# Taking half of the query-major exponentials from DMA transposes in an attention gradient kernel

## The chip, the cores and the metric

The kernel runs on one core of one Trainium2 chip. The metric is device microseconds of one execution. The kernel before takes 2852.1 us (median of 2 runs, 2850.25 to 2853.94). "PE" is the matmul engine, "DVE" the vector engine, "ACT" the activation engine, "POOL" the general one, and "SP" the engine whose queue issues the transposes. A busy DMA share can exceed 1, because it adds up the times of overlapping packets.

## The reference

The program is a forward pass and its gradients: `out = x + attention(LN(x)) * silu(mlp(LN(x)))`, with 2048 tokens, width 512, 32 heads of 16. The part that matters is the attention and its backward pass:

```
p  = softmax(q k^T / 4)          # 2048 x 2048, for each of 32 heads
o  = p v
dV = p^T do
dS = p * (do v^T - rowsum(do*o)) # the backward pass of the softmax
dQ = dS k ,  dK = dS^T q
```

The exponentials are wanted in two layouts. Sums over keys (o, dQ) need key-major tiles, with keys on the partitions. Sums over queries (dK, dV) need query-major ones. The same number is therefore wanted twice, transposed.

## The kernel before

The attention part works through 16 pairs of heads times 4 chunks of 512 queries, which makes 64 blocks of 16 steps. In a step `g`:

- PE computes key-major scores `s` (128 keys x 512 queries, two heads), and ACT computes `et = exp(s)`.
- PE computes `d`, and DVE multiplies it with `et` into `gts`. Every two steps a 512 KB DMA transpose turns `gts` into the query-major `gk`.
- For a *unit* of the block before (128 queries x 512 keys, two heads; `kc` is the group of 512 keys, `qb` the group of 128 queries), the query-major exponentials come by one of two ways. Either PE computes the transposed scores `t` and ACT a second exp, `e = exp(t)`; or a 256 KB DMA transpose of a part of `et` delivers `ek`. The list `dma_units` says which. PE then multiplies them, and `gk`, into `Z`.

```python
    dma_units = ((1, 3), (3, 3))          # (kc, qb): 2 of a block's 16 units
    lagb = 3
    ...
    ps_st = ...tc.tile_pool(name="ps_st", bufs=2, space=PSUM)   # s and t share two buffers
    etp = sb("etp", 3)
    gtp = sb("gtp", 4)
    gbp = sb("gbp", 6)                    # gk tiles, 8 KB a partition each
    ekp = sb("ekp", 4)                    # ek tiles, 2 KB a partition each
    ...
    def emit_t(g):
        b = b_unit(g)
        if b is None or b[1:] in dma_units:
            return                        # no scores and no second exp for these
        ...
    def emit_dmat(g):
        ...
        if kb % 2 == 1:
            h = (kb // 2) % 2
            if h == 0:
                blk[j]["Gk"][kc] = gbp.tile([128, 2, 16, 128], bf16, name="gk")
            nc.sync.dma_start_transpose(out=blk[j]["Gk"][kc][:, h], in_=st_gt[g][:].rearrange("k a h q -> k (a h q)"))
        if kb % 4 == 3:
            for qb in range(4):
                if (kc, qb) in dma_units:
                    ek = ekp.tile([128, 8, 128], bf16, name="ek")
                    blk[j]["Ek"][(kc, qb)] = ek
                    nc.sync.dma_start_transpose(out=ek[:], in_=st_et[g][:, qb].rearrange("k a h q -> k (a h q)"))
    ...
    def emit_z(g, part):                  # the unit of block j, one block and lagb steps later
        ...
            if (kc, qb) in dma_units:
                ev = blk[j]["Ek"].pop((kc, qb))[:].rearrange("q (a h) k -> q h a k", h=2)
            else:
                ev = st_e.pop(g)[:].rearrange("q h (a k) -> q h a k", a=4)
            for hj in range(2):
                nc.tensor.matmul(Z[...], lhsT=blk[j]["W1"][:, qb, hj, :], rhs=ev[:, hj], ...)
    ...
    for g in range(NSTEP + 16 + lagb):    # the whole loop is unrolled
        ...
        emit_t(g); emit_le(g - 1); emit_exp_b(g); emit_s(g + 1); emit_d(g)
        emit_mult(g); emit_exp_a(g + 1); emit_dmat(g); emit_g(g - 1)
        emit_z(g - lagb, 0); emit_z(g - lagb, 1)
```

## Time and profile before

| | |
|---|---|
| span of the profiled run | 2849 us |
| attention loop | 287 to about 2240 us |
| a step, a block | 1.90 us, 30.4 us |
| exps per block | 16 key-major, 14 query-major |
| DMA transposes per block | 8 gk (512 KB), 2 ek (256 KB) |
| moved by DMA in the loop | 171 GB/s, 5.2 MB a block |

The page of the kernel before gives the span in 40 slices: busy tenths of ACT and DMA, the clock granted to PE, and the GB/s moved.

```profile
ACT  2342799999999999999999999999999634440020
PEclk8898799999999999999999999999999978887989
DMA  5434889999999999999899999999999753326431
GB/s 177 107 126 128 156 161 184 159 179 172 167 180 159 181 166 174 174 164 182 156 182 171 167 183 154 183 168 170 177 164 159 191 164 103 97 83 160 115 130 42
```

ACT is at 9 tenths through the whole loop, and DMA at 8 or 9. The windows view of the kernel before has the loop as one stretch, then three half-microsecond stretches at the end of one transpose.

```profile
core 0: us, PE busy (x) PEld busy (x) DVE busy (x) ACT busy (x) POOL busy (x), PEclk, DMA share, GB/s
310.00:2230.00 1920.00, 1754.38 (x16104) 539.64 (x16098) 1540.08 (x2582) 1758.90 (x1889) 262.06 (x687) 1.00 0.98 171
...
1002.50:1003.00 0.50, 0.50 (x6) 0.10 (x4) 0.47 (x1) 0.14 (x1) 0.00 (x0) 1.00 1.10 205
1003.00:1003.50 0.50, 0.50 (x12) 0.22 (x10) 0.00 (x0) 0.50 (x1) 0.00 (x0) 1.00 0.15 28
1003.50:1004.00 0.50, 0.50 (x8) 0.11 (x2) 0.46 (x1) 0.50 (x2) 0.00 (x0) 1.00 0.00 0
```

ACT is busy for 1759 of 1920 us, and PE 1754 us. A mean DMA share of 0.98 does not mean "full", because it is 1.10 while a transpose moves data and zero between transposes. The timeline of ACT in the kernel before shows what one exp really costs (columns: start, duration, engine, line, what).

```profile
1011.08 1.05 ACT L676 ACTIVATE et<-s 128x1024 bf16<-128x1024 f32 x1
1011.99 1.06 ACT L684 ACTIVATE e<-t 128x1024 bf16<-128x1024 f32 x1
1012.89 1.07 ACT L676 ACTIVATE et<-s 128x1024 bf16<-128x1024 f32 x1
```

The starts lie 0.90 us apart although each lasts 1.06 us: consecutive exps overlap. The waits view of the loop of before (who waited for whom: us in total, times, longest) has these lines.

```profile
ACT e L684 <- PE t L634: 157.9, 254, 1.7
...
PE s L648 <- ACT et L676: 117.9, 499, 0.5
...
SPq L710 <- DVE gts L697: 1299.2, 457, 4.7
```

ACT and PE wait a little for each other. The SP queue spends most of its time waiting for `gts`, so it has room.

### The profile page before, as it was taken

Reading aid. Unit: us, or ns where it says so; the run is one execution under the profiler, and the core shown is the slowest. Engines: PE = TensorE matmul, PEld = TensorE weight load, DVE = VectorE, ACT = ScalarE, POOL = GpSimd, SP = SyncE. Lnnn points to the kernel's source line nnn. Section 1 sums busy time; section 2 is a strip of 40 time slices with the busy share of each in tenths; the row PEclk is TensorE's granted clock in tenths of the full one; section 3 lists DMA queues with packets and bytes.
Section 4 is the critical chain, followed back from the end, with each engine's and each line's share of the span. In section 5 each row is a group of like instructions: output and inputs, shape, how many; then the busy total and the mean of one; then the engine's idle time right before and its main releaser. Section 6 shows DMA issues by size and latency. Waiting matters only on the chain. (4 is left out here: it accounts for less than half of the span.)

```text
span 2849.1 us, 50869 instructions
## 1 busy us (share of the span) xinstructions
PE 2397.8 (84%) x19712; PEld 845.8 (30%) x19712; DVE 2029.7 (71%) x3382; ACT 2057.1 (72%) x2357; POOL 619.0 (22%) x1023
## 2 busy tenths in 40 slices
PE   3686999999999999999999999999999857665967
PEld 2332222222222222222222222222222333332443
DVE  5664778878878878878877877888888638880044
ACT  2342799999999999999999999999999634440020
POOL 0434101111111110101101111110101227870024
PEclk8898799999999999999999999999999978887989
DMA  5434889999999999999899999999999753326431
GB/s 177 107 126 128 156 161 184 159 179 172 167 180 159 181 166 174 174 164 182 156 182 171 167 183 154 183 168 170 177 164 159 191 164 103 97 83 160 115 130 42
DMA packets 1426198, 442.86 MB, mean 155 GB/s; under 512 B 1349281, under 2 KB 1410082, under 8 KB 1425954
## 3 DMA queue, kind: packets, MB, share of 16 engines
q1 hardware_dynamic: 1352562, 385.98, 72.9%
q10 hardware_dynamic: 73392, 53.62, 6.2%
q8 instruction: 154, 2.52, 0.3%
q14 instruction: 90, 0.74, 0.1%
HBM read 65.41 MB, written 55.32 MB: 42 GB/s over the span
## 5 line engine op out<-in xcount | busy, mean ns | idle before, releaser
L697 DVE TENSOR_TENSOR gts<-d,et 128x512 bf16<-128x512 f32 x2048 | 1315.0, 683 | 374.6 <-ACT et L676 146.4
L676 ACT ACTIVATE et<-s 128x1024 bf16<-128x1024 f32 x1024 | 1058.1, 1056 | 11.8 <-PE d L662 11.7
L684 ACT ACTIVATE e<-t 128x1024 bf16<-128x1024 f32 x896 | 933.9, 1043 | 165.0 <-PE t L634 163.9
L662 PE MATMUL d<-QDT,KVT 32*128 32x512 bf16 x2048 | 492.4, 382 | 30.5 <-DVE gts L697 28.5
L648 PE MATMUL s<-QDT,KVT 32*128 32x512 bf16 x2048 | 402.9, 385 | 135.7 <-ACT et L676 120.3
L729 PE MATMUL X<-et,Lc 128*32 128x512 bf16 x2048 | 405.3, 392 | 14.1 <-DVE xs L750 14.1
L732 PE MATMUL X<-et,NAT 128*32 128x512 bf16 x2048 | 405.5, 393 | 0.0
L744 PE MATMUL X<-gts,NAT 128*17 128x512 bf16 x2048 | 400.7, 388 | 0.0
L813 PE MATMUL Z<-gk,W 128*32 128x512 bf16 x2048 | 394.2, 379 | 0.0
L807 PE MATMUL Z<-e,W 128*32 128x512 bf16 x1792 | 351.3, 387 | 2.8 <-DVE acc L820 2.0
L634 PE MATMUL t<-KVT,QDT 32*128 32x512 bf16 x1792 | 349.9, 382 | 2.3 <-ACT e L684 2.3
L777 POOL TENSOR_TENSOR W<-NATQd,rL 128x128 bf16<-128x128 bf16 x64 | 25.7, 401 | 1386.0 <-DVE rL L772 1386.0
L648 PEld LDWEIGHTS <-KVT 32*128 32x128 bf16 x2048 | 146.9, 91 | 399.3 <-issue 397.8
L634 PEld LDWEIGHTS <-QDT 32*128 32x128 bf16 x1792 | 103.9, 91 | 365.7 <-issue 365.7
L744 PEld LDWEIGHTS <-NAT 128*17 128x17 bf16 x2048 | 93.0, 88 | 338.5 <-issue 338.5
L729 PEld LDWEIGHTS <-Lc 128*32 128x32 bf16 x2048 | 104.3, 93 | 216.2 <-issue 216.2
L820 DVE TENSOR_TENSOR acc<-Z,acc 64x512 f32<-64x512 f32 x192 | 129.0, 672 | 13.0 <-PE Z L813 13.0
L807 PEld LDWEIGHTS <-W 128*32 128x32 bf16 x2048 | 121.3, 93 | 55.3 <-issue 53.8
L662 PEld LDWEIGHTS <-KVT 32*128 32x128 bf16 x2048 | 108.1, 91 | 9.4 <-issue 1.0
L825 POOL CAST ob<-acc 64x512 bf16<-64x512 f32 x64 | 38.7, 605 | 313.3 <-DVE acc L820 311.3
L813 PEld LDWEIGHTS <-W 128*32 128x32 bf16 x2048 | 103.9, 96 | 7.5
L732 PEld LDWEIGHTS <-NAT 128*32 128x32 bf16 x2048 | 99.3, 94 | 14.5
(200 smaller groups left out, 2600.2 us busy)
## 6 DMA issues: line engine op xcount, KB each, us to landing
gk<-gts SPq DMA_TRANSPOSE x512, 4.4
HG_s<-hg SPq DMA_DIRECT2D x16, 448.0 KB, 3.0
DH_s<-dh ACTq DMA_DIRECT2D x16, 448.0 KB, 2.5
NAT<-NAT_s SPq DMA_DIRECT2D x16, 264.0 KB, 3.1
GB_s<-gB ACTq DMA_DIRECT2D x16, 256.0 KB, 2.0
dKVT_s<-ob SPq DMA_DIRECT2D x16, 256.0 KB, 3.8
dhc<-DH_s ACTq DMA_DIRECT2D x2, 2048.0 KB, 13.9
w_sb<-in_B_w_dram SPq DMA_DIRECT2D x2, 1792.0 KB, 14.8
```

Of the source, the lines that this page charges most:

```text
L634: nc.tensor.matmul(t[:, hj, :], lhsT=op["QDT"][r:r + 32, q0:q0 + 128], rhs=op["KVT"][r:r + 32, kc * 512:(kc + 1) * 512], start=True, stop= ...
L648: nc.tensor.matmul(s[:, hj, :], lhsT=op["KVT"][r:r + 32, kb * 128:(kb + 1) * 128], rhs=op["QDT"][r:r + 32, qc * 512:(qc + 1) * 512], start ...
L662: nc.tensor.matmul(d[:], lhsT=op["KVT"][r:r + 32, kb * 128:(kb + 1) * 128], rhs=op["QDT"][r:r + 32, qc * 512:(qc + 1) * 512], start=True, ...
L676: nc.scalar.activation(out=et[:, :, kb % 4, :, :].rearrange("k b h q -> k h b q"), in_=st_s.pop(g)[:].rearrange("k h (b q) -> k h b q", b= ...
L684: nc.scalar.activation(out=e[:], in_=st_t.pop(g)[:], func=ACT.Exp)
L697: nc.vector.tensor_tensor(out=gts[:, kb % 2, hj, :].rearrange("k (b q) -> k b q", b=4), in0=ds[hj][:].rearrange("k (b q) -> k b q", b=4), ...
L729: nc.tensor.matmul(X[64 + 32 * hj:96 + 32 * hj, :], lhsT=Lc[:], rhs=et[:, :, kb % 4, hj, :], start=(kb == 0), stop=False, skip_group_check ...
L732: nc.tensor.matmul(X[32 * hj:32 * hj + 32, :], lhsT=NATt[:, kb, hj, 1:33], rhs=et[:, :, kb % 4, hj, :], start=(kb == 0), stop=(kb == 15), ...
L744: nc.tensor.matmul(X[64 + 32 * hj:64 + 32 * hj + 17, :], lhsT=NATt[:, kb, hj, 0:17], rhs=gts[:, kb % 2, hj, :], start=False, stop=(kb == 1 ...
L807: nc.tensor.matmul(Z[32 * hj:32 * hj + 32, :], lhsT=blk[j]["W1"][:, qb, hj, :], rhs=ev[:, hj], start=(qb == 0), stop=False, tile_position= ...
L813: nc.tensor.matmul(Z[32 * hj:32 * hj + 32, :], lhsT=blk[j]["W2"][:, qb, hj, :], rhs=gv[:, :, :, hj, qb, :], start=False, stop=(qb == 3), t ...
L820: nc.vector.tensor_tensor(out=av, in0=Z[0:64, :], in1=av, op=ALU.add)
```

## The change

The intent is to relieve ACT, the busiest engine: 8 of 16 units instead of 2 get their exponentials from a transpose. That needs more `ek` buffers, and one `gk` buffer is given up for them.

```diff
-    dma_units = ((1, 3), (3, 3))
+    dma_units = tuple((kc, qb) for kc in range(4) for qb in (1, 3))
@@
-    gbp = sb("gbp", 6)
-    ekp = sb("ekp", 4)
+    gbp = sb("gbp", 5)
+    ekp = sb("ekp", 10)
```

## The prediction

> **What bounds the kernel now.** The span is 2849 us. The attention loop (1024 steps, 64 blocks of 16) runs from 287 to about 2240 us, so a step takes about 1.90 us and a block 30.4 us. The rest is untouched. In the windows view (310 to 2230 us) the busy shares are ACT 92%, PE 91%, DVE 80%, PEclk 1.00. ACT is the limit: consecutive exps start 0.90 to 0.92 us apart in the timeline although each lasts 1.04 to 1.06 us, and 30 exps a block take 27.3 us. In the waits view, exp b waits 158 us for its scores and scores s wait 118 us for the exp: a two-buffer ping-pong around ACT.
>
> The queue that the change loads is nearly full as well. The page gives DMA 9 tenths everywhere in the loop, 171 GB/s mean. In half-us windows the data move at 205 to 220 GB/s while a transpose is under way and at zero between; near 1004 to 1010 us three transposes in a row (1.31 MB) hold about 210 GB/s. Only short spells after a stall reach 290. So I read about 217 GB/s as what this stream of 256-byte packets sustains, about 80% used.
>
> **What the change does.** Of 16 query-major units per block, 8 instead of 2 come from transposes. Per block:
> - removed: 6 exps (5.5 us of ACT) and 12 PE matmuls for t (about 0.31 us a pair, 1.9 us). ACT falls to about 22 us. DVE (24 us) is unchanged.
> - added: 6 transposes of 256 KB, 1.57 MB. The loop moves 171 GB/s x 30.4 us = 5.2 MB per block now, 6.8 MB after.
> - moved: gk buffers 6 to 5. A gk transpose now waits about one step longer for the Z matmul that frees its buffer; it is needed 16 steps later, so this costs only queue slack.
>
> If the transposes were free, DVE would bound the loop at 25 to 26 us per block, 280 us less. But 6.8 MB at 217 GB/s is 31.2 us per block, already above 30.4, before any gap. The SP queue says the same: a gk transpose occupies it 1.93 us (median), an ek 1.80 us, issues are about 0.1 us apart, so four per group of four steps cost 7.9 us, plus operand loads (about 0.5 us per group), against 7.6 us that a group takes now. Some of these durations are the queue being held by the one before, so the two limits are not added. I expect 32 to 33.5 us per block, most likely 32.8: the limit moves from ACT to the DMA transposes, and the loop gets 2 to 3 us per block (about 150 us in all) longer.
>
> The Trainium skill, "DMA: Bandwidth & Descriptors", Latency and other measured facts, gives 261 GB/s for transposes with a non-contiguous middle dimension and more when contiguous; this trace shows about 217 sustained. If 261 held, 26 us per block would do and the change would win.
>
> **Prediction:** 3000 us, range 2910 to 3110; faster by over 2% 0.07, within 2% 0.11, slower 0.82.
>
> **What would show it.** DMA bandwidth in the loop near 205 to 215 GB/s with hardly any zero windows; ACT busy down to about 65 to 70%; gk landing later than 4.4 us; DVE's gts or ACT's exp waiting on DMA (gts or et buffers held by transposes); SP no longer waiting 1322 us for gts but issuing back to back; PE idle up.
>
> **What would make it wrong.** If 217 GB/s is only the pace of one lone transpose and a backlog flows at 290, or if ek's issue costs SP far less than 1.8 us when not held, the loop gets faster. If gk and ek issue leave gaps of 1 us each, or throttled PE lowers its clock, it is worse than 3110.

## The result, and the profile after

The kernel after takes 3129.2 us (median of 2 runs, 3126.5 to 3131.9), and before took 2852.1 us. Ratios in this document are the mean time of one kernel's fast runs over that of the other's in the same rounds, so not quite the ratio of the quoted medians. Here the ratio is 1.097, with a 95% interval of 1.094 to 1.101. The change makes the kernel 9.7% slower. I had expected 5.2%, and 3129 lies just above my range.

The same lines of the page of the kernel after:

```profile
ACT  2443676766667666666767666676767734441020
PEclk8997898989989898888989899898989987887989
DMA  5435999999999999999999999999999983324531
GB/s 175 114 125 129 196 194 195 196 196 192 196 193 194 194 194 194 191 196 194 193 198 195 193 193 193 195 194 194 189 195 197 190 226 111 105 89 134 137 123 41
```

ACT went down to 6 or 7 tenths, PE's clock lost a little, and the GB/s row is now flat at 189 to 198: the sign of a loop that runs at the pace of one steady resource. The windows view of the kernel after, for the loop:

```profile
310.00:2500.00 2190.00, 1887.09 (x15329) 484.77 (x15329) 1529.38 (x2579) 1460.69 (x1509) 262.94 (x687) 0.90 1.12 194
```

A step now takes 2.17 us and a block 34.7 us, in which 194 GB/s makes 6.7 MB. The bytes are close to the forecast (6.8 MB); the rate is not, since I had expected 205 to 215 GB/s in the loop. ACT is busy for 67% of the time. The waits view of the kernel after, for the loop, shows new waits:

```profile
DVE gts L697 <- DMA gk<-gts: 272.1, 131, 4.8
...
ACT e L684 <- PE t L634: 548.0, 396, 5.7
ACT et L676 <- DMA ek<-et: 82.3, 74, 2.7
...
SPq L710 <- PE d L662: 336.3, 156, 3.5
SPq L710 <- DVE gts L697: 273.3, 196, 3.3
```

DVE and ACT now wait for transposes to have read their buffers (`gts` and `et`), which no line of before says. SP's wait for `gts` shrank from 1299 to 273 us. A new wait of SP for PE appeared, at the line that issues the gk transpose: that line has to wait for a free gk buffer. It looks like a cause in its own right, and the experiments take it up. The timeline of SP in the kernel after shows how its queue is filled:

```profile
1036.46 3.68 SPq L716 DMA_TRANSPOSE ek<-et  x2
1040.24 4.38 SPq L710 DMA_TRANSPOSE gk<-gts  x2
1044.72 3.22 SPq L716 DMA_TRANSPOSE ek<-et  x2
1048.03 2.28 SPq L594 DMA_TRANSPOSE KVT<-KVPad  x1
1050.41 5.84 SPq L710 DMA_TRANSPOSE gk<-gts  x2
```

(`KVT` is an operand of the next pair of heads.) Each line begins about 0.1 us after the one before has ended. To see where the stream's time goes, I sorted the packets of the trace into slices of 0.1 us by the rate of the 256-byte transpose packets, and counted us per block (from the trace, worked out over the loop):

```
                          before   after
burst, over 250 GB/s        2.8     4.6
180 to 250 GB/s (mean 216) 17.4    20.9
20 to 180 GB/s (mean 130)   3.6     5.7
plain copies                0.8     0.7
trickle, about 10 GB/s      1.9     2.1
nothing at all              4.0     0.8
sum                        30.4    34.7
```

The idle time of 4.0 us a block has been used up, down to 0.8. What stays are dips, a trickle, and bursts. The trickle was in the kernel before too, where 4.0 idle us a block stood beside it; whether it cost anything there no run tested. These are its windows in the kernel after, half a microsecond each:

```profile
1012.50:1013.00 0.50, 0.50 (x3) 0.10 (x2) 0.31 (x1) 0.00 (x0) 0.00 (x0) 0.50 0.97 193
1013.00:1013.50 0.50, 0.50 (x6) 0.11 (x4) 0.40 (x2) 0.28 (x1) 0.00 (x0) 0.50 4.68 126
1013.50:1014.00 0.50, 0.50 (x8) 0.11 (x4) 0.43 (x3) 0.50 (x1) 0.23 (x1) 0.53 0.02 2
1014.00:1014.50 0.50, 0.50 (x12) 0.22 (x10) 0.41 (x2) 0.50 (x2) 0.50 (x3) 1.00 0.09 9
1014.50:1015.00 0.50, 0.50 (x8) 0.10 (x3) 0.50 (x2) 0.50 (x1) 0.50 (x3) 1.00 0.83 96
1015.00:1015.50 0.50, 0.41 (x3) 0.09 (x1) 0.50 (x2) 0.39 (x2) 0.50 (x2) 1.00 1.27 290
```

The rate (last column) falls from 193 to 2 GB/s for about a microsecond and comes back as a burst at 290. Just before, one 16 KB packet of the queue that the profile calls "instruction" began. Over all 120 such packets in the loop of after, the mean transpose rate in half-microsecond slices, from 2 us before a packet's start to 4 us after it, is (worked out from the trace):

```
us from start   -2   -1.5  -1   -0.5   0    0.5   1    1.5   2    2.5   3    3.5
GB/s           194   206  189   186  138    29   11    97  251   258  245   219
```

Of the 2.8 us a block of trickle and of nothing at all in after, about 2.0 us lie within 1.6 us after such a start (worked out from the trace). Each packet lasts 0.95 us (median). They are PE's instructions being fetched: 148 packets of 16,384 bytes are 2.42 MB, which is 64 bytes for each of PE's 2 x 18,944 matmuls and weight loads. The Trainium skill, "Runtime: NRT & Kernel Launch", Instruction fetch mechanics, says that an engine's instructions are fetched in 16 KiB blocks over a DMA queue of the engine's own, and calls the cost "mostly hidden". The block size agrees. Whether the cost is hidden is for the experiments. A second instruction queue (q14, packets of 8 KB, about 67 in the loop of after) shows a smaller dip, from about 200 GB/s to 80 for half a microsecond; no run varied it.

### The profile page after: what moved, and what is told of

Read it like the earlier page. It is cut to its first block, busy times and chain, and to the rows that moved or that the text cites. A ratio compares the mean times of both kernels' runs of the same rounds, so it can differ in the third digit from the quotient of the medians.

```text
span 3130.1 us, 49097 instructions
## 1 busy us (share of the span) xinstructions
PE 2535.6 (81%) x18944; PEld 791.9 (25%) x18944; DVE 2021.1 (65%) x3382; ACT 1755.6 (56%) x1973; POOL 621.0 (20%) x1023
## 3 DMA queue, kind: packets, MB, share of 16 engines
q8 instruction: 148, 2.42, 0.3%
## 5 line engine op out<-in xcount | busy, mean ns | idle before, releaser
L676 ACT ACTIVATE et<-s 128x1024 bf16<-128x1024 f32 x1024 | 1016.4, 1025 | 189.3 <-DMA ek<-et 82.3
L684 ACT ACTIVATE e<-t 128x1024 bf16<-128x1024 f32 x512 | 523.5, 1023 | 570.6 <-PE t L634 559.2
L662 PE MATMUL d<-QDT,KVT 32*128 32x512 bf16 x2048 | 617.6, 415 | 264.5 <-DVE gts L697 262.0
L729 PE MATMUL X<-et,Lc 128*32 128x512 bf16 x2048 | 441.7, 428 | 12.5 <-DVE xs L750 12.3
L744 PE MATMUL X<-gts,NAT 128*17 128x512 bf16 x2048 | 437.6, 423 | 0.0
L813 PE MATMUL Z<-gk,W 128*32 128x512 bf16 x2048 | 436.6, 420 | 0.0
L807 PE MATMUL Z<-e,W 128*32 128x512 bf16 x1024 | 221.6, 426 | 10.6 <-ACT e L684 7.3
L634 PE MATMUL t<-KVT,QDT 32*128 32x512 bf16 x1024 | 219.1, 425 | 0.0
L807 PE MATMUL Z<-ek,W 128*32 128x512 bf16 x1024 | 218.3, 423 | 0.0
L634 PEld LDWEIGHTS <-QDT 32*128 32x128 bf16 x1024 | 48.8, 92 | 234.7 <-issue 234.7
```

The lines of the kernel that those rows point to most:

```text
L634: nc.tensor.matmul(t[:, hj, :], lhsT=op["QDT"][r:r + 32, q0:q0 + 128], rhs=op["KVT"][r:r + 32, kc * 512:(kc + 1) * 512], start=True, stop= ...
L662: nc.tensor.matmul(d[:], lhsT=op["KVT"][r:r + 32, kb * 128:(kb + 1) * 128], rhs=op["QDT"][r:r + 32, qc * 512:(qc + 1) * 512], start=True, ...
L676: nc.scalar.activation(out=et[:, :, kb % 4, :, :].rearrange("k b h q -> k h b q"), in_=st_s.pop(g)[:].rearrange("k h (b q) -> k h b q", b= ...
L684: nc.scalar.activation(out=e[:], in_=st_t.pop(g)[:], func=ACT.Exp)
L729: nc.tensor.matmul(X[64 + 32 * hj:96 + 32 * hj, :], lhsT=Lc[:], rhs=et[:, :, kb % 4, hj, :], start=(kb == 0), stop=False, skip_group_check ...
L744: nc.tensor.matmul(X[64 + 32 * hj:64 + 32 * hj + 17, :], lhsT=NATt[:, kb, hj, 0:17], rhs=gts[:, kb % 2, hj, :], start=False, stop=(kb == 1 ...
```

## The experiments

Four theories stood against each other. **Volume:** the loop runs at what the stream of transposes sustains. **Buffers:** the cut from 6 to 5 gk buffers, or the ring of waits through it, costs the time. **Clock:** PE was granted less clock, 0.90 instead of 1.00 in the loop, and this slows the loop. **Instructions:** the SP queue's cost for each transpose, not its bytes, is the limit. Every time below stands against before in the same rounds (2851.6 to 2853.1 us medians). After is 3129 us.

### e1: the gk buffer put back

```diff
-    gbp = sb("gbp", 5)
+    gbp = sb("gbp", 6)       # on the kernel after
```

> The kernel after with the gk buffers put back from 5 to 6. Theory volume (the loop runs at the pace of the DMA transposes, 6.8 MB a block): the stream is idle at zero bandwidth for only 0.8 us of a block's 34.7 us, so at most 52 us are to be had: 3075 to 3130 us. Theory buffers (the queue's 530 us of waiting for Z matmuls to free a gk buffer is what costs the time): below 3000 us. Theory clock (PE's granted clock fell from 1.00 to 0.89): 3129 us.

Measured: 3126.0 us, ratio 1.096 (1.094 to 1.099). The waits of SP in this run:

```profile
SPq L710 <- DVE gts L697: 683.7, 376, 8.1
...
SPq L716 <- PE d L662: 103.4, 115, 2.4
```

The wait of the gk issue for PE is gone from the list (a shorter one stands at the ek issue, L716), and the wait for `gts` has grown from 291 to 684 us over the whole run. The queue waits for something else instead, and the time is the same. The wait was a symptom.

### e2: the kernel before with one gk buffer less

```diff
-    gbp = sb("gbp", 6)
+    gbp = sb("gbp", 5)       # on the kernel before
```

> The kernel before with 5 gk buffers instead of 6, nothing else. Theory volume: 2845 to 2880 us, since a gk transpose is needed 16 steps after it could start. Theory buffers: over 2910 us. Theory clock: 2852 us.

Measured: 2849.0 us, ratio 1.000 (0.998 to 1.002). The buffer costs nothing on this side either. The buffer theory is out.

### e3: the six transposes added, but no work saved

```diff
-    dma_units = tuple((kc, qb) for kc in range(4) for qb in (1, 3))
+    dma_units = ((1, 3), (3, 3))
+    issue_units = tuple((kc, qb) for kc in range(4) for qb in (1, 3))
...
-                if (kc, qb) in dma_units:      # in emit_dmat
+                if (kc, qb) in issue_units:
```

> The kernel after's 8 ek transposes per block are all issued, with its buffers, but only before's two replace an exp; the six others are read by nobody, and ACT and PE do all of before's work. Theory volume: as slow as the kernel after or a little slower, 3120 to 3200 us, with PE's clock back near 1.00 because PE has its t matmuls. Theory clock: PE as busy as before keeps its clock, so under 2950 us. A theory that the lost time is a dependence of the Z matmuls on the ek tiles: also under 2950 us, since nobody reads them.

Measured: 3131.7 us, ratio 1.098 (1.096 to 1.101), which is the kernel after's time. Nobody reads the six added `ek` tiles here, and ACT and PE do all the work of before. The time of the kernel after is thus the time of its transposes, and neither the saved exps nor the new reads matter. The windows view of this run for the loop:

```profile
310.00:2500.00 2190.00, 1944.53 (x16062) 530.19 (x16060) 1533.89 (x2575) 1787.49 (x1884) 263.25 (x687) 0.91 1.12 194
```

One expectation failed: the clock did not come back. It is 0.91 even with all the t matmuls done. All of before's matmuls are spread over 14% more time here, which fits a clock that follows how densely PE works.

### e4: the work saved, but no transposes added

Six of the eight units read a stale `ek` tile, so the gradients of K and V are wrong on purpose.

```diff
+    issue_units = ((1, 3), (3, 3))             # transposed; dma_units is still all eight
-    ekp = sb("ekp", 10)
+    ekp = sb("ekp", 4)
...
-                ev = blk[j]["Ek"].pop((kc, qb))[:]....
+                ev = blk[j]["Ek"][(1, 3) if kc < 2 else (3, 3)][:]....
```

> The kernel after without its six added transposes: 8 units per block skip their exp and t matmuls, two are transposed, the six others read one of those two (wrong dK/dV on purpose). Theory volume: the loop is then bound by DVE at 25 to 26.5 us per block, 2540 to 2630 us, DMA at the 5.2 MB per block of before. Theory clock: PE's clock falls as in the kernel after and the loop stays above 2750 us.

Measured: 2786.3 us, ratio 0.978 (0.975 to 0.980). This misses what I expected, 2540 to 2630 us, and also lies above 2750 us, the mark of the clock theory; but PE was granted its full clock here (1.00 below), so that theory does not explain it. The windows view of this run for 500 us of the loop, and two lines of its waits view for 310 to 2100 us:

```profile
1000.00:1500.00 500.00, 464.86 (x4136) 126.87 (x4138) 408.70 (x695) 388.03 (x406) 73.30 (x190) 1.00 1.00 177
...
ACT e L685 <- PE t L635: 398.6, 485, 2.2
...
PE d L663 <- DVE gts L698: 110.6, 488, 0.4
```

ACT fell to 78%, but PE stands at 93% and DVE at 82%, and a step takes 1.84 us instead of 1.90. With six of the fourteen second exps gone, ACT's `e` waits for PE's `t` for 399 of 1790 us. PE itself waits for DVE's `gts` for 111 us, and its wait for ACT's `et` (118 us in before) is no longer in the list. So PE is now as busy as ACT was in before, and the trace points to PE as the next limit; no run tested this. Even free of charge the change could have won only 66 us.

### e5 to e8: dose, size and count of the transposes

The merged version takes units qb 2 and 3, whose parts of `et` lie side by side, in one transpose of 512 KB.

```diff
 e5 (after, same bytes, 12 transposes a block instead of 16)
-    dma_units = tuple((kc, qb) for kc in range(4) for qb in (1, 3))
+    dma_units = tuple((kc, qb) for kc in range(4) for qb in (2, 3))
+            ek = ekp.tile([128, 2, 8, 128], bf16, name="ek")            # ekp: 5 of these
+            nc.sync.dma_start_transpose(out=ek[:]..., in_=st_et[g][:, 2:4].rearrange("k b a h q -> k (b a h q)"))
 e6   dma_units = tuple((kc, 3) for kc in range(4))                      # 4 units, gbp 6, ekp 6
 e7   dma_units = all eight but (0, 1) and (2, 1)                        # 6 units, gbp 5, ekp 9
 e8   the kernel after, and the other 8 units transposed into tiles that nobody reads
```

> The kernel after with units qb 2 and 3 instead of 1 and 3, so that the two ek transposes of a group become one of 512 KB: the same bytes, 12 transposes a block instead of 16. Theory bytes (the stream's 216 GB/s plus stalls that come per us of stream): 3080 to 3130 us. Theory instructions (each transpose costs the queue about 2 us whatever its size, dips between transposes): 4 fewer of 16, 2750 to 2900 us, bound by the compute loop.

> 4 transposed units per block (qb 3 of each group) with 6 gk and 6 ek buffers. 5.7 MB a block. Theory bytes: at the 195 GB/s that the loop of after sustains 29.3 us a block, which is under the 29.4 us of the run without the added transposes and under before's 30.4; the two limits are close and not quite hidden: 2800 to 2880 us. A theory that every added transpose costs its share at once (277 us for 6): 2852 + 92 = 2944 us.

> 6 transposed units per block, otherwise after's buffers (ek 9). 6.2 MB a block at 195 GB/s is 32.0 us: 2950 to 2990 us by theory bytes, that is after minus 2 x 64 x 1.35 us. If the loss has a step (a ring that closes only at 8 units), below 2900 us.

> The kernel after with all 16 units transposed, eight of them into tiles that nobody reads. Theory bytes: each 262 KB costs 1.35 us (at 195 GB/s) while the loop is bound by the stream, 8 x 64 x 1.35 = 690 us: 3780 to 3860 us. If the queue's issue limits (1.32 us for an ek behind an ek, hidden in the stream when it is full), less than 3700.

| run | ek per block | measured us | ratio (95%) |
|---|---|---|---|
| before | 2 | 2853.1 | 1 |
| e6 | 4 | 2855.6 | 1.000 (0.998 to 1.002) |
| e7 | 6 | 2960.0 | 1.037 (1.035 to 1.039) |
| after | 8 | 3129.2 | 1.097 (1.094 to 1.101) |
| e8 | 16 | 3836.3 | 1.344 (1.342 to 1.346) |
| e5 | 8, in 4 merged | 3073.3 | 1.077 (1.075 to 1.079) |

This is a knee and then a straight line. From 2 to 4 the time stays. From 6 to 8 each ek costs (3129.2 - 2960.0) / 2 = 85 us, and from 8 to 16 it costs 707 / 8 = 88 us. Over 64 blocks that is 1.32 and 1.38 us for 262 KB, or 190 to 198 GB/s: the rate of the loop. The volume theory said 1.35 us beforehand. The merged version moves the same bytes and is 56 us faster, so the count of transposes matters too, but as a small part: 0.22 us for each transpose less. The instruction theory in its strong form (2750 to 2900 us) is out. Of the ranges for theory bytes, those of e6, e7 and e8 held, and e5 came out 7 us below its own. The slices by rate agree that a transpose has a small cost of its own: the time at 20 to 180 GB/s is 5.7 us a block with 16 transposes (after), 4.8 with 12 (e5), 3.6 with 8 (e11, below) and 8.5 with 24 (e8). All these transposes go through SP's one queue; whether that queue or the DMA engines behind it set the rate was not tested.

### e9, e10 and e13: the instruction fetches

`X` is the tile in which PE adds up the sums over keys, with six matmuls a step.

```diff
 e9 (after, 16 empty PE instructions in every step)
+        for _ in range(16):
+            nc.tensor.nop(nofuse=True)
 e10 (after, no X matmuls in steps 1 to 14 of a block; wrong results on purpose)
+        if 0 < kb < 15:
+            return                              # in emit_le, before its matmuls into X
-        for hj in range(2):                     # in emit_g, its matmuls into X
+        for hj in range(2 if kb in (0, 15) else 0):
 e13 (after, eight one-column matmuls that add zeros; results correct)
+        for i in range(8):
+            hj = i % 2
+            nc.tensor.matmul(X[64 + 32 * hj:80 + 32 * hj, 0:1], lhsT=Lc[:, 0:16], rhs=et[:, 0, kb % 4, hj, 0:1],
+                             start=False, stop=False, ...)
```

> The kernel after with 16 empty instructions on PE in every step, which do nothing but have to be fetched: about 65 more 16 KB instruction fetches than after's 148. Theory fetch (each such packet holds one DMA engine for about 1 us, the transposes on all 16 trickle meanwhile, and about half is caught up in the burst that follows): 0.5 to 1.1 us each, 3160 to 3205 us, and more time at a trickle. Theory that fetches are harmless: 3129 us, if the empty instructions fit into PE's idle time.

> The kernel after without the X matmuls of steps 1 to 14 of each block (wrong results on purpose): 10,752 fewer PE instructions, about 42 fewer fetches, DMA work unchanged. Theory fetch: 20 to 45 us less than after, 3084 to 3110 us. Theory that PE's speed or clock has a hand in it: below 3050 us. Neither: 3129 us.

> The kernel after with eight added one-column matmuls of zeros per step (16 instructions with their weight loads, correct results): about 64 more 16 KB fetches. Theory fetch: 0.5 to 1.1 us each, as e10's 28 us for 42 fewer: +35 to +70 us, 3164 to 3200 us, and trickle time up from 2.07 to about 3.2 us a block. Theory that fetches are harmless and e10 gained by less PE work: the added PE work is small (an estimate of 0.1 us each, within PE's idle time), so 3129 to 3140 us with fetches at about 212.

The line of the "instruction" queue that carries PE's fetches (packets, MB, share), in after, e9, e10 and e13:

```profile
q8 instruction: 148, 2.42, 0.3%
```
```profile
q8 instruction: 148, 2.42, 0.3%
```
```profile
q8 instruction: 106, 1.74, 0.2%
```
```profile
q8 instruction: 212, 3.47, 0.4%
```

e9 measured 3130.3 us and tells nothing of fetches: they are still 148, and its trace has no added PE instruction, so the empty instructions were not in the program that ran. It serves as a repeat of after in the rounds of e10. e10 measured 3101.9 us (ratio 1.088, 1.086 to 1.089): 42 fetches less and 27 us less than after, 0.65 us each. e13 measured 3180.4 us (1.114, 1.113 to 1.116): 64 fetches more and 51 us more, 0.80 us each. The trickle fell from 2.07 to 1.55 us a block in e10 and rose to 2.91 in e13; over 64 blocks that is 33 us less and 54 us more, which fits both changes. e10 also takes PE work away and e13 adds some, so neither is pure; e10 also frees `et` and `gts` of readers. That both give the same size per fetch, and that the trickle moves by as much, makes the fetch the likely cause.

e10 also speaks against the clock. Its windows view for 500 to 2000 us:

```profile
500.00:2000.00 1500.00, 1377.52 (x6954) 246.81 (x6955) 1057.37 (x1783) 1020.13 (x1045) 182.81 (x475) 0.65 1.10 197
```

PE was granted 0.65 of its clock, far less than the 0.90 of after, and the kernel was faster, though with less PE work. The dose runs agree: an ek cost 85 us while the clock went from 0.96 (e7) to 0.90, and 88 us while it went from 0.90 to 0.74 (e8), so the falling clock added next to nothing. The Trainium skill, "TensorE: Matmul & The Clock Gate", Part 1, has the clock throttled by default and released by activity. The fewer matmuls PE runs in the same 1500 us, the lower the clock (12,606 matmuls and 1.00 in before, 10,479 and 0.90 in after, 7954 and 0.74 in e8, 6954 and 0.65 here). The runs give no sign that the lower clock costs time in this loop.

### e11, e12 and e14: fewer, larger transposes

The two gk transposes of a group become one of 1 MB as well; `gts` tiles then hold four steps (3 buffers of twice the size). All three runs have 5 gk buffers; e12 and e14 have 3 ek buffers of twice the size.

```diff
-        if kb % 2 == 0:
-            cur["gts"] = gtp.tile([128, 2, 2, 512], bf16, name="gts")
+        if kb % 4 == 0:
+            cur["gts"] = gtp.tile([128, 4, 2, 512], bf16, name="gts")
...
-        if kb % 2 == 1:                         # two transposes of 512 KB
+        if kb % 4 == 3:                         # one of 1 MB
+            blk[j]["Gk"][kc] = gbp.tile([128, 2, 16, 128], bf16, name="gk")
+            nc.sync.dma_start_transpose(out=blk[j]["Gk"][kc][:]..., in_=st_gt[g][:]...)
 e11  on e5: 8 units, 8 transposes a block
 e12  dma_units = tuple((kc, qb) for kc in (1, 3) for qb in (2, 3))     # 4 units, 6 transposes
 e14  dma_units = ((3, 2), (3, 3))                                      # 2 units, 5 transposes
```

> e5 with the two gk transposes of a group merged into one of 1 MB as well (gts tiles of four steps): the same bytes in 8 transposes a block instead of 12. e5 gave 56 us for 4 fewer, 0.22 us each. Theory dip (a fixed loss at each boundary between transposes): 3073 - 56 = 3015 to 3030 us. Theory that only small transposes pay: 3070 us. It may be slower if a 1 MB transpose starts too late for its buffers.

> Four units per block, qb 2 and 3 of groups 1 and 3, their ek transposes merged in twos and the gk ones too: 5.7 MB in 6 transposes a block instead of 10 for before. Theory bytes plus dips: the stream needs about 27.5 us a block, so it is no longer the limit; ACT has two exps less than before: 2790 to 2840 us, which would beat both kernels by 1 or 2%. If the gk transposes' later start starves the gts buffers: above 2852 us.

> e12's merging with before's number of transposed units, two (qb 2 and 3 of group 3): before's bytes in 5 transposes a block instead of 10. If before is bound by ACT alone, merging gives it nothing: 2840 to 2860 us, and e12's gain needs the four units. If merging alone makes e12's gain: 2790 to 2800 us.

e11 measured 3041.0 us (ratio 1.067, 1.064 to 1.069). Merging gk gave another 32 us, 0.13 us for each transpose less: below the 0.22 of e5, so the expectation was a little too good. e14 measured 2825.6 us (0.990, 0.988 to 0.992) and e12 measured 2796.3 us (0.982, 0.979 to 0.984). Results are correct in all three. e12 beats both kernels. About half of its gain comes with the merging alone (e14), which I had not expected for before's two units; the rest comes from the four units, which without merging gave nothing (e6). e14 fell between its two expected ranges, so before was not bound by ACT alone: e14 has as many exps. e14 also moves one unit and changes buffer numbers, so its 27 us are not the merging's alone beyond doubt. The windows view of e12 for the loop:

```profile
310.00:2150.00 1840.00, 1693.93 (x15653) 506.25 (x15653) 1519.43 (x2550) 1635.32 (x1742) 259.98 (x678) 0.99 1.10 194
```

ACT is at 89%, PE at 92%, and DMA at the same 194 GB/s as after, with fewer bytes to move. That is below the 203 GB/s that the merged transposes of e11 sustain. Why merging helps before's two units, where the stream is idle part of the time, I did not test.

## Why the prediction was wrong, and where it was right

- **Right: what bounds the loop of the kernel after.** It is the stream of transposes. That ACT alone was the limit of before is not shown: PE was as busy, six exps a block less gave only 66 us (e4), and e14 gained 27 us with as many exps. The forecast of 6.8 MB per block held, ACT fell to 67%, DVE and ACT came to wait for transposes, and SP's wait for `gts` shrank. e3 shows it best: the transposes alone, with nothing saved, take the kernel after's time.
- **Right: the buffer cut costs only slack.** e1 and e2 show no effect.
- **Wrong: the size of the DMA term. This is the step that failed.** "I expect 32 to 33.5 us per block, most likely 32.8": it was 34.7. I had divided the bytes by 217 GB/s, which gave a floor of 31.2 us. The stream does run at a mean of 216 GB/s in the slices of 180 to 250, which is how these are picked; over all its slices of 20 GB/s and more the mean is 208, and over the whole loop, plain copies included, 194. I gave 1.6 us for everything that interrupts it, and the interruptions cost 3.5 us, net of what the bursts make up. Two of them have a measured size. Instruction fetches cost 0.65 to 0.80 us each (e10, e13), and 120 of them in 64 blocks make 1.2 to 1.5 us a block. The dip at each transpose costs 0.13 to 0.22 us (e5, e11), and sixteen of them a block make 2.1 to 3.5 us (an estimate, since only the merging of eight was measured). Together that is 3.3 to 5.0 us, which covers the 3.5. 1.9 us too little in 64 blocks is 122 us, nearly all of the 129 us by which 3000 missed 3129. I had seen the stalls and the bursts at 290 in the trace of before, but did not ask what caused the stalls or what they would cost once there was no idle time left to hide them. The two reasons that I had named for a time over 3110 us do not explain it: the gaps in the queue are 0.1 us, not 1 us, and PE's clock did fall, but no run shows that this cost time.
- **Wrong: the gain to be had.** "If the transposes were free, DVE would bound the loop at 25 to 26 us per block, 280 us less." e4 gave 66 us and 29.4 us a block. I took DVE's busy time as the next limit and passed over PE, which was busy for 91% of the loop. I had counted on PE being relieved of 1.9 us a block; its busy time in e4 is 27.3 us a block, against 27.8 in before. Why so little was saved is open. This did not move the number that I forecast, since the transposes hid it, but it would have mattered for any smaller dose.
- **Wrong in its size: the queue's own reading.** I took 1.80 us of SP for an ek. In after an ek right behind another takes 1.32 us (median from the trace). Much of the 1.80 was the queue being held by the data before it. I had left room for that by not adding the two limits.
- **The skill's 261 GB/s** ("DMA: Bandwidth & Descriptors", Latency and other measured facts) was rightly not used for this loop. It sustained 194 GB/s with its transposes of 256 and 512 KB (after), 200 with all of 512 KB (e5), and 203 with those of 512 KB and 1 MB (e11).

## What to carry to other kernels

Before moving work from a busy engine to DMA, count the bytes per iteration and divide by the rate that the trace shows over whole iterations at full load, with its stalls and dips, and not by the rate inside one transfer: here interruptions that stood beside 4.0 idle us a block before became a cost when the queue was full. A cheap test is to add the new transfers without using them, and another to remove the work without the transfers; here these gave +9.8% and -2.2%, and so named the limit and the most that could be won. When a queue waits for a buffer, give the buffer back and look at the time before believing the wait. Where DMA transposes are the limit, try merging them first: here it gave 56 and then 32 us.

## What the Trainium skill lacked or had wrong

- "Runtime: NRT & Kernel Launch", Instruction fetch mechanics, calls the cost of a 16 KiB fetch "mostly hidden". That is not so for the transposes of this unrolled kernel. Around a fetch the transposes fall from about 190 to 11 GB/s for about a microsecond, and in the DMA-bound loop a fetch costs 0.65 to 0.80 us (e10, e13; the likely cause, as both runs also change PE's work).
- "DMA: Bandwidth & Descriptors" says nothing of instruction fetches slowing a stream of DMA transposes. Here trickle and empty slices within 1.6 us after the start of one of the loop's 120 make about 2.0 us in a block of 34.7 us.
- The same page gives transposes 261 GB/s with a non-contiguous middle dimension and more when contiguous. These transposes from on-chip memory to on-chip memory ran at a mean of 208 GB/s while running (slices of 20 GB/s and more; 216 in those of 180 to 250), reached 290 only in bursts after a stall, and sustained 194 to 203 GB/s.
- The same page gives no figure for what one more transpose costs in a full stream of them. Merging showed 0.22 us (256 KB pairs into 512 KB) and 0.13 us (512 KB pairs into 1 MB).
